# Four casts moved from VectorE to ScalarE, and three bias products moved ahead of a transpose, in the start-up of an attention-and-mixer kernel

## Chip, cores, metric

One core of a Trainium2 chip (trn2). The metric is the device time of one execution in microseconds (us), slowest core, here the only one. Lower is better.

## The reference

T5-style attention with a relative-position bias, then a mixer whose token mixing is low rank. Eight batches, eight heads, 576 tokens, head size 64; rank 32; hidden width 2048.

```python
def _attn_ref(q, k, v, bias_table):            # (8, 8, 576, 64)
    scores = scale * np.matmul(q, k.transpose(0, 1, 3, 2))
    ...                                        # bucket of |i - j|, 32 buckets
    scores = scores + bias.transpose(2, 0, 1)[None]
    attn = softmax(scores)                     # shortened
    return np.matmul(attn, v)

def _moe_ref(x, U, V, w_ch1, w_ch2):           # x: (8, 576, 512)
    h = x.transpose(0, 2, 1) @ U @ V           # U: 576 x 32, V: 32 x 576
    u = x + h.transpose(0, 2, 1)
    return u + np.maximum(u @ w_ch1, 0.0) @ w_ch2
```

## The kernel before

The kernel works through 32 "pairs" (batch, two heads). The bias is applied as a product after the exponential: `P = exp(scale * q k)` on ScalarE, then `P *= eb` on VectorE near the diagonal, where `eb` is a table of exponentiated biases that GpSimd (or VectorE) writes in reversed order. U and V are cast into zero-padded bf16 tiles `upad` and `vpad`. Batch 0 (pairs 0 to 3) is scheduled by hand, as the start-up is; from pair 4 on, score work is interleaved with the channel matmuls of earlier batches (the "dense" part). In all timelines shown here each engine's instructions stand in the order in which they are emitted.

```python
def cast_uv():                                   # the mixing weights
    nc.vector.tensor_copy(out=upad[:, 0:4, 0:R], in_=u_st[:, 0:4, :])
    for par in range(2):
        rows = slice(par * 64, par * 64 + 64)
        nc.vector.tensor_copy(out=upad[rows, 4 + par, 0:R], in_=u_st[rows, 4, :])
    nc.vector.tensor_copy(out=vpad[0:R, 0:S], in_=v_st)

# ... GpSimd's queue, in order
    load_w1(0)                                   # 1 MB with a cast on the way
    load_rem(1, 0)
    load_rem(1, 1)
    qk1 = [[load_pair(which, 0) for which in range(2)]]

    def more_loads():
        for pr in (2, 3):
            load_eb(pr)
        reverse_eb(2, nc.gpsimd.tensor_copy)     # table of pair 2
        load_w1(1)
        reverse_eb(3, nc.gpsimd.tensor_copy)     # table of pair 3
        # ... pair 1 of batch 1, v of batch 1, pairs 2 and 3, then load_w2 twice

# ... slot 1 and its neighbours
    kts(1, 2)                                    # a score tile of pair 1, with its exponential
    kts(1, 3)
    pvs(0, 4, 0, 1, 2, 3)                        # value products of pair 0 (PE)
    bands(1, 4, 0)                               # bias products of pair 1 (VectorE)
    cast_uv()
    normalise(0)
    rem_scores(2)
    kts(2, 0)
    first_transposes(3, qk0.pop(3), one)         # PE, then two copies on VectorE
    bands(1, 1, 2)
    first_rem_transposes(3)
    bands(1, 3)
    mix_t(0, nc.scalar.copy)                     # first reader of upad
    kts(2, 1)
    pvs(1, 4, 0, 1)
    kts(2, 2)
    pvs(1, 2, 3)
    ...
    bands(2, 4, 0, 1, 2, 3)

# batch 2's loads (GpSimd): remainders, then q and k in turn, then v
        for t in range(NKT):
            for which in range(2):
                seq.append(lambda which=which, t=t: main(which, t))
```

The softmax here doesn't subtract the row's maximum and nothing guards it: scores larger than these inputs give would overflow.

## Time and profile before

| | before |
|---|---|
| time, three runs | 409.25 us (408.82 to 409.63) |
| span of the profiled run | 407.1 us |
| PE idle in 24 to 30 us | 0.33 + 1.01 us |
| first dense slot (pair 4's first score matmul) | 38.47 us |
| PE waits for batch 2's q load | until 69.77 us, 0.52 us |

How to read it: PE is busy 95% of the time, so only PE's waits are worth anything. The views that carry this are in the prediction. Some lines that it names without showing them follow: GpSimd's timeline, VectorE's product of pair 2, the third exponential of pair 2 on ScalarE and PE's first dense slot (start, duration, engine, line, operation, output and inputs; in brackets the idle time before and its releaser).

```profile
27.72 0.74 POOL L265 DMA_DIRECT2D qb<-in_k_dram  x1 [4.37 <-DMA w1b<-in_moe_w_ch_dram]
28.46 0.84 POOL L213 COPY eb<-stage 128x768 bf16<-128x768 bf16 x1
...
28.06 1.57 DVE L587 TENSOR_TENSOR p_sb<-p_sb,eb 128x256 bf16<-128x256 bf16 x1
...
26.24 1.02 ACT L533 ACTIVATE p_sb<-sc 128x1024 bf16<-128x1024 f32 x1 [0.81 <-PE sc L524]
...
38.47 0.39 PE L537 MATMUL sc<-qkT 128*128 128x128 bf16 x4
```

GpSimd stands still for 4.37 us until the first half of `w1b` has landed, then issues one load, and only then makes the table for pair 2.

### The profile page before, as it was taken

How to read it: one execution, taken by the hardware profiler on the slowest of the kernel's cores; microseconds unless marked ns; L12 is line 12 of the kernel's file. 1: busy time of each engine (PE TensorE's matmuls, PEld its weight loads, DVE VectorE, ACT ScalarE, POOL GpSimd, SP SyncE). 2: the span in 40 equal slices, each digit the busy share in tenths (PEclk: the TensorE clock that was granted, in tenths of full speed). 3: DMA queues.
4: the chain of work that ended last, by engine and by line, in shares of the span. 5: the costliest groups of instructions: out<-in, count | busy, mean ns of one | idle time of the engine just before them, and what ended most of it. 6: DMA issues, size and time to landing. Idle time of an engine off the chain costs nothing.

```text
span 407.1 us, 9061 instructions
## 1 busy us (share of the span) xinstructions
PE 386.2 (95%) x3636; PEld 214.7 (53%) x3700; DVE 245.5 (60%) x558; ACT 205.7 (51%) x285; POOL 125.1 (31%) x179
## 2 busy tenths in 40 slices
PE   3889999999999999999999999999999999999995
PEld 1456555555555555555555555555555554444443
DVE  6987887758655675556755776558656832422321
ACT  4877644665654566556655665555554640220310
POOL 4958924454454045404540454040000000000000
PEclk9789999999999999999999999999999999999999
DMA  7999999999999699949996999499032003001012
GB/s 130 178 163 162 111 191 120 124 101 156 157 83 105 132 120 83 131 103 143 100 105 130 136 80 97 101 138 102 14 66 66 14 14 101 30 7 72 25 27 78
DMA packets 162754, 40.68 MB, mean 100 GB/s; under 512 B 151792, under 2 KB 157176, under 8 KB 162712
## 3 DMA queue, kind: packets, MB, share of 16 engines
q0 software_dynamic: 108416, 17.97, 61.1%
q1 hardware_dynamic: 53080, 21.22, 25.7%
q10 hardware_dynamic: 1216, 0.92, 0.8%
q8 instruction: 29, 0.48, 0.5%
q14 instruction: 13, 0.11, 0.1%
HBM read 37.84 MB, written 9.45 MB: 116 GB/s over the span
## 4 chain that ended last, share of the span: by engine, by line
PE 81%; DMA 11%; POOL 5%; issue 2%; DVE 1%; ACT 0%; DVEq 0%; POOLq 0%
PE acc L392 30%; PE acc L372 27%; PE o L611 10%; PE sc L524 7%; DMA w1b<-in_moe_w_ch_dram 4%; DMA w2b<-in_moe_w_ch_dram 3%; PE acc L647 2%; POOL v_bf L255 2%; PE acc L663 1%; POOL qb L265 1%; DMA qb<-in_q_dram 1%; PE sc L537 1%; PE sc L558 1%; DMA tblT<-in_bias_table_dram 1%; DMA gp_dram<-gp 1%
## 5 line engine op out<-in xcount | busy, mean ns | idle before, releaser
L533 ACT ACTIVATE p_sb<-sc 128x1024 bf16<-128x1024 f32 x128 | 124.5, 1021 | 100.9 <-PE sc L524 100.7
L392 PE MATMUL acc<-w2b,g 128*128 128x512 bf16 (+1 forms) x560 | 128.6, 373 | 2.3 <-DVE ob L401 0.5
L372 PE MATMUL acc<-uT,w1b 128*128 128x512 bf16 x484 | 116.3, 380 | 2.5 <-issue 0.6
L392 PEld LDWEIGHTS <-g 128*128 128x128 bf16 x592 | 55.1, 98 | 70.2 <-issue 11.7
L372 PEld LDWEIGHTS <-w1b 128*128 128x128 bf16 x576 | 53.2, 98 | 71.5 <-issue 13.1
L383 DVE TENSOR_SCALAR g<-acc 128x512 bf16<-128x512 f32 x94 | 64.7, 690 | 34.7 <-PE acc L372 31.7
L587 DVE TENSOR_TENSOR p_sb<-p_sb,eb 128x768 bf16<-128x768 bf16 (+3 forms) x160 | 71.1, 473 | 10.1 <-ACT p_sb L533 9.5
L381 ACT ACTIVATE g<-acc 128x512 bf16<-128x512 f32 x50 | 29.9, 598 | 59.9 <-PE acc L372 59.7
L611 PEld LDWEIGHTS <-p_sb 128*128 128x128 bf16 x1600 | 56.1, 98 | 7.0 <-issue 1.3
L611 PE MATMUL o<-v_bf,p_sb 128*128 128x65 bf16 x1500 | 58.0, 194 | 0.3 <-DVE p_sb L587 0.3
L401 DVE TENSOR_TENSOR ob<-acc,u_tok 128x512 f32<-128x512 f32 x32 | 22.1, 691 | 44.3 <-PE acc L392 41.7
L524 PE MATMUL sc<-qkT 64*128 64x512 bf16 x256 | 41.4, 392 | 1.2 <-ACT qkT L469 0.7
L915 POOL COPY gate<-xp 1x2 bf16<-1x2 bf16 x18 | 3.2, 176 | 121.5 <-DVE xp L636 121.5
L671 DVE TENSOR_TENSOR u_tok<-acc,xp 128x512 bf16<-128x512 f32 x32 | 22.1, 691 | 24.8 <-PE acc L663 24.7
L636 DVE TENSOR_TENSOR xp<-o,rcp 128x320 bf16<-128x320 f32 x60 | 29.5, 492 | 3.2
L255 POOL DMA_DIRECT2D v_bf<-in_v_dram x32 | 28.5, 914 | 1.9 <-DMA w1b<-in_moe_w_ch_dram 1.5
L255 POOL DMA_DIRECT2D qb<-in_k_dram x24 | 21.7, 906 | 5.5 <-DMA w2b<-in_moe_w_ch_dram 3.5
L255 POOL DMA_DIRECT2D qb<-in_q_dram x24 | 22.0, 915 | 4.7 <-DVE u_tok L671 4.7
L567 ACT ACTIVATE p_sb<-sc 128x640 bf16<-128x640 f32 x32 | 22.3, 698 | 0.2
L550 ACT ACTIVATE p_sb<-sc 128x512 bf16<-128x512 f32 x32 | 19.1, 597 | 4.7 <-PE sc L537 3.4
L634 DVE RECIPROCAL rcp<-o 128x5 f32<-128x5 f32 x60 | 11.4, 191 | 12.2 <-PE o L611 11.5
L647 PEld LDWEIGHTS <-upad 128*128 128x128 bf16 x160 | 11.4, 98 | 7.7 <-DVE xp L636 0.7
(90 smaller groups left out, 257.9 us busy)
## 6 DMA issues: line engine op xcount, KB each, us to landing
out_dram<-ob SPq DMA_DIRECT2D x32, 256.0 KB, 2.3
v_bf<-in_v_dram POOLq DMA_DIRECT2D x32, 128.0 KB, 5.8
qb<-in_q_dram POOLq DMA_DIRECT2D x27, 128.0 KB, 4.4
qb<-in_k_dram POOLq DMA_DIRECT2D x27, 128.0 KB, 4.4
w1b<-in_moe_w_ch_dram POOLq DMA_DIRECT2D x2, 1024.0 KB, 8.9
w2b<-in_moe_w_ch_dram POOLq DMA_DIRECT2D x2, 1024.0 KB, 12.1
stage<-gp_dram SPq DMA_DIRECT2D x4, 192.0 KB, 4.4
qkT<-qb SPq DMA_TRANSPOSE x40, 4.9
```

The lines of the kernel that those rows point to most:

```text
L255: nc.gpsimd.dma_start(out=dst, in_=src[b, :, t * 128 : (t + 1) * 128, :].rearrange("h p d -> p h d"),)
L372: nc.tensor.matmul(gp_, lhsT=w1b[:, ct, nt * 128 : (nt + 1) * 128], rhs=rhs[:, ct, :], start=(ct == 0), stop=(ct == 3),)
L381: nc.scalar.activation(g[:, nt, :], gp_, AF.Relu)
L383: nc.vector.tensor_relu(out=g[:, nt, :], in_=gp_)
L392: nc.tensor.matmul(op[:, c0:c1], lhsT=g[:, nt, tt * 128 : (tt + 1) * 128], rhs=w2b[:, nt, c0:c1], start=(nt == 0), stop=(nt == NHT - 1), s ...
L401: nc.vector.tensor_tensor(out=ob[:, c0:c1].rearrange("p (a c) -> p a c", c=128), in0=op[:, c0:c1].rearrange("p (a c) -> p a c", c=128), in ...
L524: nc.tensor.matmul(sp[:, hh, :], lhsT=kT[rows, i * 128 : (i + 1) * 128], rhs=qT[rows, 0:S0], start=True, stop=True,)
L533: nc.scalar.activation(P[:, i, :, 0:S0], sp, AF.Exp, scale=scale)
L567: nc.scalar.activation(P4[:, 0:SP], sp.rearrange("p a c -> p (a c)")[:, 0:SP], AF.Exp, scale=scale,)
L587: nc.vector.tensor_tensor(out=t, in0=t, in1=e, op=ALU.mult)
L611: nc.tensor.matmul(o[:, qt * 66 : qt * 66 + 65], lhsT=lhs[:, c0 : c0 + 128], rhs=rhs, start=(kt == NKT and qt == 0), stop=(kt == NKT - 1), ...
L636: nc.vector.tensor_tensor(out=xo[:, :, hh], in0=o[:, :, 0:64], in1=rbc, op=ALU.mult)
```

## The change

Intent: relieve VectorE in slot 1. The casts go to ScalarE, which has a hole there, and the rest of pair 1's bias products no longer wait behind the copies of pair 3's transposes.

```diff
     def cast_uv():
-        nc.vector.tensor_copy(out=upad[:, 0:4, 0:R], in_=u_st[:, 0:4, :])
+        nc.scalar.copy(out=upad[:, 0:4, 0:R], in_=u_st[:, 0:4, :])
         for par in range(2):
             rows = slice(par * 64, par * 64 + 64)
-            nc.vector.tensor_copy(out=upad[rows, 4 + par, 0:R], in_=u_st[rows, 4, :])
-        nc.vector.tensor_copy(out=vpad[0:R, 0:S], in_=v_st)
+            nc.scalar.copy(out=upad[rows, 4 + par, 0:R], in_=u_st[rows, 4, :])
+        nc.scalar.copy(out=vpad[0:R, 0:S], in_=v_st)
@@
     kts(1, 3)
+    cast_uv()
     pvs(0, 4, 0, 1, 2, 3)
     bands(1, 4, 0)
-    cast_uv()
     normalise(0)
     rem_scores(2)
     kts(2, 0)
+    bands(1, 1, 2, 3)
     first_transposes(3, qk0.pop(3), one)
-    bands(1, 1, 2)
     first_rem_transposes(3)
-    bands(1, 3)
```

## The prediction

> **What bounds the kernel now.** I read the page first: busy shares, the 40 slices, the chain that ended last.
>
> ```profile
> PE 386.2 (95%) x3636; PEld 214.7 (53%) x3700; DVE 245.5 (60%) x558; ACT 205.7 (51%) x285; POOL 125.1 (31%) x179
> PE   3889999999999999999999999999999999999995
> PE 81%; DMA 11%; POOL 5%; issue 2%; DVE 1%; ACT 0%; DVEq 0%; POOLq 0%
> ```
>
> TensorE (PE) is busy 95% of the 407.1 us span and carries 81% of the chain; VectorE (DVE), which the change relieves, carries 1%, ScalarE (ACT) 0%. So removing vector work is worth only what PE waits for it. Those waits can lie only where PE has gaps, so I read the busy table by windows next (columns: window, length, then busy us with instruction count of PE, PEld, DVE, ACT and POOL, then clock, DMA share, GB/s).
>
> ```profile
> 18.00:21.00 3.00, 3.00 (x48) 2.56 (x48) 2.93 (x11) 1.73 (x2) 3.00 (x6) 0.50 1.68 213
> 21.00:24.00 3.00, 2.80 (x41) 1.89 (x38) 1.92 (x6) 2.06 (x3) 2.29 (x4) 0.74 1.18 214
> 24.00:27.00 3.00, 2.67 (x57) 1.93 (x57) 2.61 (x7) 2.13 (x4) 0.00 (x0) 1.00 1.36 192
> 27.00:30.00 3.00, 1.99 (x20) 1.07 (x18) 2.94 (x6) 2.79 (x5) 2.28 (x4) 1.00 1.59 104
> 70.00:200.00 130.00, 128.47 (x1326) 72.97 (x1348) 84.54 (x192) 77.05 (x105) 54.24 (x78) 1.00 1.16 118
> ```
>
> From 70 us on PE is 99% busy (128.47 of 130). The changed code lies in slot 1, where pair 1 is weighted while pair 2's scores run: about 18 to 27 us. There PE is idle 0.2 us of 21 to 24 and 0.33 us of 24 to 27, with a further 1.0 us in 27 to 30. That is the whole local stake. From 18 to 21 the granted clock is 0.50, so PE is saturated on slow matmuls there.
>
> Third, the timelines of single engines around it. ScalarE, then VectorE, then TensorE (start, duration, what; in brackets the idle time before and its releaser):
>
> ```profile
> 17.80 1.94 ACT L533 ACTIVATE p_sb<-sc 128x1024 bf16<-128x1024 f32 x2
> 21.94 0.60 ACT L550 ACTIVATE p_sb<-sc 128x512 bf16<-128x512 f32 x1 [2.21 <-PE sc L537]
> ...
> 20.18 0.31 DVE L340 CAST upad<-u_st 128x128 bf16<-128x128 f32 x1
> 20.32 0.41 DVE L343 CAST upad<-u_st 64x32 bf16<-64x32 f32 x2
> 20.76 0.57 DVE L344 CAST vpad<-v_st 32x576 bf16<-32x576 f32 x1
> 21.26 0.17 DVE L634 RECIPROCAL rcp<-o 128x5 f32<-128x5 f32 x1
> ...
> 23.59 1.29 DVE L469 COPY qkT<-acc 128x512 bf16<-128x512 bf16 x2 [1.01 <-PE acc L465]
> 24.80 1.02 DVE L587 TENSOR_TENSOR p_sb<-p_sb,eb 128x768 bf16<-128x768 bf16 x2
> ...
> 25.40 0.32 PE L611 MATMUL o<-v_bf,p_sb 128*128 128x65 bf16 x5 [0.33 <-DVE p_sb L587]
> ```
>
> The reader sees three things: ScalarE has a hole of 2.21 us just where the four casts would go; VectorE sits idle 1.01 us ahead of the transposes' copies while three bias products wait behind them; and one PE wait of 0.33 us is for exactly such a product.
>
> Last, the chain of waits in order of time, 36 to 75 us, and the PE line where it returns to PE:
>
> ```profile
> 47.29 14.17 DMA w2b<-in_moe_w_ch_dram
> 61.46 0.30 issue
> 61.76 2.60 POOL qb L255 x3
> 64.36 5.37 DMA qb<-in_q_dram
> 69.72 0.05 issue
> ...
> 69.77 0.23 PE L498 MATMUL acc<-ident,qb 128*128 128x128 bf16 x1 [0.52 <-DMA qb<-in_q_dram]
> ```
>
> This is the decisive view. The chain ahead of 69.77 us is not PE at all: it runs through the GpSimd load queue (w1b, then v and qb loads, w2b, then batch 2's q), all the way back to the start. PE reaches batch 2's first transposes 0.52 us too early and waits for a load. Whatever PE gains before that point is waited away there, unless the load comes earlier too.
>
> **What the Trainium skill says.** (1) "ScalarE: Activation LUTs", section "What ACT_TABLE_LOAD costs": an activation with immediate scale and bias takes 186 ns plus 0.833 ns per element, consecutive ones overlap by about 93 ns. The trace agrees within 3%: 128x1024 from PSUM takes 1021 ns (formula 1039), 128x512 takes 597 (612). (2) Same page, "Table sets: the hidden batching unit": copy is in every set, so these casts should need no table switch between exponentials. The trace already mixes CAST and exp on ScalarE at 24 us (0.27 us, no gap). (3) "SBUF — State Buffer", "Who interferes with whom": a VectorE instruction with two SBUF inputs contends with a GpSimd instruction that reads SBUF, and the later one blocks. The trace is consistent: a 128x256 product that takes 0.28 us elsewhere lasts 1.57 us from 28.06, beside GpSimd's table copy from 28.46.
>
> **The change, part by part.**
> 1. *Casts off VectorE.* They occupy 20.18 to 21.33, 1.15 us. But the next VectorE instruction, the reciprocal of pair 0, needs head 0 of the value product, whose last matmuls end at 20.69 + 0.47 = 21.16 on PE. It started at 21.26. So about 0.1 us comes free, not 1.15.
> 2. *Casts onto ScalarE.* By the skill's formula (an estimate; no such cast from SBUF is in the trace): 128 elements 0.29, twice 32 elements 0.21, 576 elements 0.67, together 1.38, less three overlaps of 0.09 = 1.1 us. Queued after pair 1's exponentials they run from 19.74 to about 20.9 and end 1 us ahead of 21.94, when ScalarE's next work is released by PE. Cost on the path: 0. Their first reader, pair 0's mixing on PE, comes at 23.60.
> 3. *Three bias products ahead of pair 3's copies.* They start when pair 0's normalisation lets VectorE go, about 22.4, and last 1.02 + 0.48 less one overlap of 0.08 = 1.42 us, so end about 23.85. The copies wait for PE until 23.59 anyway; they move from 23.59 to 23.85, 0.26 us later, and end about 25.15; the small remainder copy ends about 25.35 instead of 26.0. Pair 3's scores need both only at 27.6.
> 4. *PE.* Its value products of pair 1 come at 24.30, 24.46, 24.61, 24.77, so the next without a wait is at 24.93, not 25.40: 0.47 us gained (idle plus restart). Pair 2's third score tile moves from 25.81 to 25.34, its exponential from 26.24 to 25.77 (the one before ends at 25.43). The 0.81 us hole before it on ScalarE shrinks to 0.35.
> 5. *What is left at the dense stage.* From 27.4 to 35 ScalarE is nearly solid, and would pass the 0.47 on. But pair 2's bias products need the table that GpSimd reverses at 28.46 to 29.30, released by the weight load that landed at 27.44; they run from 29.55 and cannot move ahead of about 29.35. They, pair 3's products and the two normalisations behind them keep about 0.2 us. The first dense slot, at 38.47 now, should start 0.2 to 0.4 us earlier; I take 0.25.
> 6. *At 69.77.* The load's landing doesn't depend on any of this, so PE arrives 0.25 us earlier and waits 0.77 instead of 0.52. Sum at the end: about 0. I put 0.15 us down for the chance that some of it survives: 409.25 - 0.15 = 409.1 us.
>
> **The rivals.** *The gain survives*: the load's chain shifts with PE, since one releaser in it (u_tok at 56.9, ahead of the load at 57.20) is VectorE work. For: it is on record as a wait of 4.7 us. Against: that releaser is no input of a q load, and w2b is what the next wait (3.5 us) names. Then 0.25 to 0.47 us stay: 408.8 to 409.0. *A new wait on ScalarE*: the landing of v_st isn't shown; if it came late, the casts would hold pair 2's exponentials. For: SyncE issued it only at 13.2 to 13.8. Against: VectorE read it at 20.76 without waiting, so ScalarE would end by 21.5 at worst. A delay of up to half a microsecond would be soaked up by the same wait at 69.77, so 409.2 to 409.5. *GpSimd is held*: the products move from 24.8, where GpSimd is idle, to 22.4, beside its DMA issues of 20.99 to 23.35. Against: it waits 4.37 us straight after, until 27.72, so a few tenths are lost in that. Also 409.2. *The delayed copies bind*: slack above 2 us, ruled out.
>
> **Range and chances.** All paths lie within half a microsecond, 0.12%; the three runs before spread over 0.8 us (408.82 to 409.63), and run-to-run variation of load landings and of PE's clock ramp is larger than the effect. Range 408.4 to 409.8. Over 2% either way (8 us) has no mechanism: 0.5% each.
>
> **What would show it.** Right: four short ScalarE casts between 19.7 and 21.1; the two-copy line at about 23.85 with no idle second before; no PE wait for p_sb at 25; third exponential near 25.8; first dense slot near 38.2; a PE wait for batch 2's qb load near 69.8 grown to about 0.8 us, PE in step with the kernel before afterwards. Wrong: that load lands earlier or the wait is gone and the span drops by 0.3 us or more (step 6 fails); casts past 21.94 (step 2); dense slot not earlier at all (step 5).

## The result, and the profile after

| | before | after |
|---|---|---|
| median (range) of 6 runs each | 409.5 us (408.82 to 410.27) | 409.25 us (408.49 to 409.94) |
| ratio after / before | | 0.9994, 95% interval 0.9978 to 1.0011 |
| span of the profiled run | 407.1 us | 408.0 us |
| first dense slot | 38.47 us | 38.59 us |
| PE waits for batch 2's q load | until 69.77, 0.52 us | until 70.68, 1.30 us |

A ratio is the mean time of one kernel's runs over that of the other's of the same rounds, so it is not quite the ratio of the medians. No change can be told from zero. Nor can a small one be ruled out: this interval, from 0.9 us faster to 0.5 us slower, would hide all of the 0.25 to 0.48 us that were at stake. What became of them must be read from the traces and the experiments.

The page's busy shares and chain after:

```profile
PE 386.7 (95%) x3636; PEld 214.8 (53%) x3700; DVE 243.2 (60%) x554; ACT 207.0 (51%) x289; POOL 124.7 (31%) x179
...
PE 81%; DMA 10%; POOL 5%; issue 2%; DVE 1%; ACT 0%; ACTq 0%; POOLq 0%
```

VectorE has four instructions fewer and ScalarE four more, the casts (1.3 us more of work there). The chain is what it was. ScalarE's timeline in slot 1, after, VectorE's below it, and PE's fifth group of value products of pair 1:

```profile
19.30 0.31 ACT L340 CAST upad<-u_st 128x128 bf16<-128x128 f32 x1
19.49 0.46 ACT L343 CAST upad<-u_st 64x32 bf16<-64x32 f32 x2
19.98 0.67 ACT L344 CAST vpad<-v_st 32x576 bf16<-32x576 f32 x1
21.64 0.60 ACT L550 ACTIVATE p_sb<-sc 128x512 bf16<-128x512 f32 x1 [0.99 <-ACT vpad L344]
...
25.63 1.02 ACT L533 ACTIVATE p_sb<-sc 128x1024 bf16<-128x1024 f32 x1 [0.32 <-PE sc L524]
...
22.16 1.42 DVE L587 TENSOR_TENSOR p_sb<-p_sb,eb 128x768 bf16<-128x768 bf16 x3
23.49 1.28 DVE L469 COPY qkT<-acc 128x512 bf16<-128x512 bf16 x2
27.45 0.28 DVE L587 TENSOR_TENSOR p_sb<-p_sb,eb 128x256 bf16<-128x256 bf16 x1
29.79 2.00 DVE L587 TENSOR_TENSOR p_sb<-p_sb,eb 128x512 bf16<-128x512 bf16 x3 [2.05 <-POOL eb L213]
...
24.80 0.32 PE L611 MATMUL o<-v_bf,p_sb 128*128 128x65 bf16 x5
```

Locally everything happened as intended. The casts sit in ScalarE's hole and end 0.99 us ahead of its next work. The third exponential of pair 2 moved from 26.24 to 25.63. (Not all of these 0.61 us are the change's: this trace runs ahead of the other already before the changed code has an effect on PE. PE's value products of pair 0 start at 18.20 against 18.50, those of pair 1 still at 24.18 against 24.30. Within the latter the fifth group starts 0.62 us behind the first, 24.80 - 24.18, where it was 1.10, 25.40 - 24.30. So 0.48 us are the change's.) In the busy table, the window of slot 1 is now solid on PE; the one after is as empty as it was:

```profile
24.00:27.00 3.00, 3.00 (x62) 2.09 (x60) 1.75 (x6) 2.50 (x4) 0.00 (x0) 1.00 1.43 187
27.00:30.00 3.00, 1.98 (x19) 1.07 (x18) 0.91 (x4) 2.91 (x5) 1.81 (x3) 1.00 1.30 88
```

Then it is lost. VectorE, ready at 27.73 for pair 2's remaining products, waits 2.05 us for GpSimd's table. GpSimd's timeline after, and the PE lines of the first dense slot and of the first wait for a load:

```profile
28.18 0.74 POOL L265 DMA_DIRECT2D qb<-in_k_dram  x1 [5.11 <-DMA w1b<-in_moe_w_ch_dram]
28.92 0.83 POOL L213 COPY eb<-stage 128x768 bf16<-128x768 bf16 x1
...
38.59 0.39 PE L537 MATMUL sc<-qkT 128*128 128x128 bf16 x4
70.68 0.23 PE L498 MATMUL acc<-ident,qb 128*128 128x128 bf16 x1 [1.30 <-DMA qb<-in_q_dram]
```

The gain meets two gates one after the other: the table of pair 2, made behind the load of `w1b`, and then batch 2's q load. Each is on GpSimd's queue; neither was touched.

### The profile page after: what moved, and what is told of

Read it like the earlier page. It is cut to its first block, busy times and chain, and to the rows that moved or that the text cites. A ratio compares the mean times of both kernels' runs of the same rounds, so it can differ in the third digit from the quotient of the medians.

```text
span 408.0 us, 9061 instructions
## 1 busy us (share of the span) xinstructions
PE 386.7 (95%) x3636; PEld 214.8 (53%) x3700; DVE 243.2 (60%) x554; ACT 207.0 (51%) x289; POOL 124.7 (31%) x179
## 4 chain that ended last, share of the span: by engine, by line
PE 81%; DMA 10%; POOL 5%; issue 2%; DVE 1%; ACT 0%; ACTq 0%; POOLq 0%
PE acc L392 30%; PE acc L372 27%; PE o L611 10%; PE sc L524 7%; DMA w1b<-in_moe_w_ch_dram 5%; DMA w2b<-in_moe_w_ch_dram 4%; PE acc L647 2%; POOL v_bf L255 2%; POOL qb L265 1%; PE acc L663 1%; DMA qb<-in_q_dram 1%; PE sc L537 1%; PE sc L558 1%; POOL qb L255 1%; DMA gp_dram<-gp 1%
## 5 line engine op out<-in xcount | busy, mean ns | idle before, releaser
L587 DVE TENSOR_TENSOR p_sb<-p_sb,eb 128x768 bf16<-128x768 bf16 (+3 forms) x160 | 69.8, 465 | 12.1 <-ACT p_sb L533 9.5
```

Source lines behind the costliest of these rows:

```text
L587: nc.vector.tensor_tensor(out=t, in0=t, in1=e, op=ALU.mult)
```

## The experiments

Twelve kernels, all giving the right result, each timed in five rounds against the kernel before on the same chip; the lines marked "L" shift by a few where a kernel has more lines. The three groups ran on three chips: compare within a group.

The theory: PE's work in the start-up doesn't set the time, because GpSimd's load chain does, at 70 us; and the change's local gain is already waited away at pair 2's table. Rivals: the gain is kept and noise hides it; one half of the change cancels the other; PE's work sets the end and nothing was gained at all.

### The kernel before, against itself

> The kernel before, unchanged, timed against itself: ratio 1.000, and the width of the interval is the noise that every other verdict is read against. It also gives a second trace: the theory (batch 2's q load, not PE, sets the time at 69.8 us) expects the same wait of PE for that load, with a landing that wanders by some tenths from run to run; the rival (that wait was an accident of one trace) expects it gone in some traces.

Measured: 409.75 us (before 409.8), ratio 1.0000 (0.9986 to 1.0013). So nothing below about 0.13% can be seen in these times, and where an interval is wider, nothing below its width. Its second trace (VectorE line, then PE line):

```profile
29.93 2.00 DVE L587 TENSOR_TENSOR p_sb<-p_sb,eb 128x512 bf16<-128x512 bf16 x3 [2.24 <-POOL eb L213]
70.63 0.23 PE L498 MATMUL acc<-ident,qb 128*128 128x128 bf16 x1 [1.13 <-DMA qb<-in_q_dram]
```

In this trace PE's clock was at full speed throughout slot 1, and the third exponential ran at 25.59, as early as in the trace after. The kernel before, too, then stands at the table and at the q load. The later landing in the trace after (70.68 against 69.77) needs no change to explain it: the kernel before shows it too (70.63).

### The change again

> The change, unchanged: ratio 0.9985 to 1.0005. The trace after showed the first dense slot at 38.59 us against 38.47 before although slot 1 had won 0.6 us on PE, because pair 2's bias products waited for GpSimd's table until 29.79. Theory: again a VectorE wait for that table of about 2 us near 27.5, and a PE wait for the q load near 70 us. Rival (the gain is kept and only that trace hid it): dense slot at 38.0 or earlier and the time 0.3 us or more below.

Measured: 410.34 us, ratio 1.0006 (0.9991 to 1.0022). The ratio lies a hair above the 0.9985 to 1.0005 that was expected, well within its interval; the trace isn't as expected. It fell in an execution whose first loads came late: PE waited for v until 20.81, its clock fell to 0.50 between 21 and 27 us, pair 1 was slow, and the first dense slot came at 40.61, later than the table would have allowed. In that trace no wait for the q load is left near 70 us. (The 0.6 us on PE that the expectation names are 0.48, as worked out above.) So the expectation of a 2 us wait for the table was a miss for this execution. It taught something else: a start-up later by 2 us cost the span (408.6 us) only 0.6 us against the other trace of the change.

### Only the casts

```diff
     kts(1, 3)
+    cast_uv()                                   # on ScalarE
     pvs(0, 4, 0, 1, 2, 3)
     bands(1, 4, 0)
-    cast_uv()                                   # on VectorE
```

> Only the four casts moved to ScalarE, the old order of products and transposes kept. Theory: they fill a hole on ScalarE and free about 0.1 us on VectorE ahead of a reciprocal that waits for PE; PE still waits 0.3 us for the product at 25.4; third score exponential still near 26.2; time within 0.1%. Rival (the casts were the costly part): exponential 0.5 us or more earlier.

Measured: 409.75 us, ratio 1.0003 (0.9987 to 1.0019). The PE line of the product in slot 1:

```profile
24.57 0.32 PE L611 MATMUL o<-v_bf,p_sb 128*128 128x65 bf16 x5 [0.32 <-DVE p_sb L587]
```

PE still waits 0.32 us there, as expected. The third exponential came at 25.41, and not near 26.2; taken alone that is what the rival forecast (0.5 us or more earlier). But this trace's clock was at 0.96 to full speed from 18 us on, where that of the kernel before had 0.50 and 0.74 until 24, and the kernel before, traced again at full speed, had it at 25.59 with no cast moved. So the spacing is compared, not the moment: the third exponential follows the first by 25.41 - 22.18 = 3.23 us, against 3.15 in the kernel before (26.24 - 23.09), 3.22 in its second trace (25.59 - 22.37) and 2.73 with the whole change (25.63 - 22.90). The casts alone don't help slot 1. The first dense slot was at 38.36, no later than with the whole change: slot 1's gain doesn't reach it.

### Only the order

```diff
     kts(2, 0)
+    bands(1, 1, 2, 3)
     first_transposes(3, qk0.pop(3), one)
-    bands(1, 1, 2)
     first_rem_transposes(3)
-    bands(1, 3)
```

> Only the bias products moved ahead of pair 3's transposes, casts left on VectorE. Theory: this half holds the whole local gain, PE's wait at 25 us gone, third exponential near 25.8 (0.45 us earlier); then VectorE waits for the table of pair 2, dense slot within 0.25 us of before, time within 0.1%. Rival (the delayed copies of pair 3 bind): scores of pair 3 later than 27.6 and the time longer.

Measured: 409.64 us, ratio 0.9998 (0.9981 to 1.0015). The time fits. The profiled execution was again one with late first loads (clock 0.50 in 24 to 27 us, first dense slot at 41.19), so the expected 25.8 of the exponential can't be checked. PE's wait for the product is gone in it (but at half the clock the products had more time). That this half holds the local gain rests on the difference between the whole change and the casts alone.

### Useless work on PE

Two, or fourteen, 512-column matmuls that nobody reads, just ahead of the first dense slot of the kernel before:

```diff
+    pad = acc()
+    for _ in range(2):                          # 14 in the second kernel
+        nc.tensor.matmul(pad, lhsT=ident, rhs=vpad[:, 0:S0], start=True, stop=True)
     put_off = [lambda g=g: mix_h(g) for g in range(NPAIR)]
```

> The kernel before with two useless 512-column matmuls (0.22 us each, about 0.43 us) on PE just ahead of the first dense slot. Theory (PE waits 0.5 to 1.3 us for batch 2's q load at 69.8): they come out of that wait, time within 0.1 us. Rival (PE work alone sets the end): 0.43 us longer.

> The same with fourteen such matmuls, 3.0 us. Theory: the wait at 69.8 us takes 0.5 to 1.3 us of it, the rest is seen: 1.7 to 2.5 us longer, and the wait for the q load is gone. Rival: 3.0 us longer.

Measured: two matmuls 409.4 us, ratio 0.9999 (0.9982 to 1.0016); fourteen 410.76 us, ratio 1.0039 (1.0025 to 1.0053), which is 0.0039 x 409.5 = 1.6 us for 3.0 us of work. PE lines: the wait that is left with two, then the padding with fourteen. Below them GpSimd's issue of batch 2's last q load with fourteen.

```profile
70.43 0.23 PE L498 MATMUL acc<-ident,qb 128*128 128x128 bf16 x1 [1.31 <-DMA qb<-in_q_dram]
...
38.49 3.19 PE L895 MATMUL acc<-vpad,ident 128*128 128x512 bf16 x14
...
64.54 0.90 POOL L255 DMA_DIRECT2D qb<-in_q_dram  x1
```

With two, the time can't decide: its interval, 0.7 us each way, is wider than the dose of 0.43. Fourteen settle the rival that PE's work alone sets the end: 3.0 us longer would be 1.0073, outside the interval. About 1.4 of the three microseconds vanish, and no wait for the q load near 70 us is left. They also answer the prediction's first rival, that the load's chain shifts with PE: with PE 3 us later from 38.49 on, the last q load was issued at 64.54, against 64.36 in the kernel before and 64.92 with two. (The VectorE instruction that is named as the releaser in that chain changes from trace to trace: u_tok, p_sb, g.) A PE time saved before 70 us is waited away there as long as that wait stands: the same wait, seen from the other side. (1.6 is a little under the 1.7 to 2.5 that was expected; the slack in these executions is at the upper end, and the interval is 0.6 us each way.)

### The q loads of batch 2 ahead of its k loads

```diff
-        for t in range(NKT):
-            for which in range(2):
-                seq.append(lambda which=which, t=t: main(which, t))
+        pairs = [(which, t) for t in range(NKT) for which in range(2)]
+        if b == 2:
+            pairs.sort()
+        for which, t in pairs:
+            seq.append(lambda which=which, t=t: main(which, t))
```

> The kernel before with batch 2's four q loads issued ahead of its four k loads (same loads, same bytes). The last q load is issued some 2.6 us earlier (three loads of 0.87 us). Theory: PE's wait for it, 0.5 to 1.3 us, goes, and the time drops by about that, 0.4 to 1.0 us; k lands about a microsecond later than it did, still ahead of its transposes 3 us on. Rival (another wait lies just behind): time within 0.2 us.

> The same reordering on top of the change. Theory: with the load out of the way the change is worth what the first dense slot gains: between 0 and 0.3 us below the reordered kernel before, since the table of pair 2 holds VectorE until about 29.5. Rival (the change's 0.5 us in slot 1 lasts once the load is gone): 0.5 us below it.

Measured: on the kernel before 408.61 us, ratio 0.9986 (0.9971 to 1.0001); on the change 408.57 us, ratio 0.9983 (0.9969 to 0.9997). PE in the second one, where it used to wait:

```profile
68.81 0.39 PE L500 MATMUL acc<-ident,qb 128*128 128x128 bf16 x4
69.03 0.22 PE L500 MATMUL acc<-ident,rem 128*128 128x128 bf16 x1
```

The wait is gone in this trace, and about 0.6 to 0.7 us of time with it; with the change on top the interval just excludes 1, without it it just includes it. (The trace without the change again had late first loads, first dense slot 40.20, so that it can't show the wait gone.) The two kernels can't be told apart, 0.04 us between the medians, which fits the theory that the first gate still stands; but with intervals of 0.6 us each way the times don't exclude the rival's 0.5 us. In the trace of the second one GpSimd's table started at 28.50 and the first dense slot came at 38.35, as in the kernels without this edit.

### The tables of pairs 2 and 3 made earlier

GpSimd makes both tables ahead of its loads for pair 0 of batch 1, when it would otherwise soon stand still, not after them.

```diff
-    qk1 = [[load_pair(which, 0) for which in range(2)]]
+    qk1 = []
     def more_loads():
         for pr in (2, 3):
             load_eb(pr)
         reverse_eb(2, nc.gpsimd.tensor_copy)
-        load_w1(1)
         reverse_eb(3, nc.gpsimd.tensor_copy)
+        qk1.append([load_pair(which, 0) for which in range(2)])
+        load_w1(1)
```

> The kernel before with GpSimd reversing the tables of pairs 2 and 3 ahead of the loads of pair 0 (at about 21 us), not behind the weight load that lands near 27.5. Theory: pair 2's products start when VectorE is free (about 28), not at 29.5 to 29.9, and GpSimd issues the second half of w1b about 0.8 us earlier, so the load chain behind it moves ahead too: PE's wait near 70 us shrinks by about that; time 0.3 to 1.0 us below. Rival (the load queue's room, not GpSimd's instructions, sets the landings): wait near 70 unchanged, time within 0.2 us.

> The same on top of the change. Theory: with the table there, slot 1's 0.5 us is no longer waited away near 27.5; dense slot at 37.5 to 38.1 in a trace whose clock comes up early; but the q load's wait near 70 us takes it, so the time is that of the early-table kernel before within 0.3 us. Rival (the table was the only thing that hid the gain): 0.5 us below it.

Measured: on the kernel before 410.6 us, ratio 1.0027 (1.0009 to 1.0046), that is 1.1 us slower; on the change 409.22 us, ratio 1.0002 (0.9986 to 1.0018). The first is a clear miss. Its VectorE line and its PE line in slot 1:

```profile
20.21 2.36 DVE L343 CAST upad<-u_st 64x32 bf16<-64x32 f32 x1
...
24.80 0.48 PE L647 MATMUL acc<-xp,upad 128*128 128x128 bf16 x5 [1.40 <-DVE xp L636]
```

A 64x32 cast that takes 0.18 to 0.19 us in the kernel before lasts 2.36 us here. It ends at 22.57, with GpSimd's two table copies, which run from 20.87 to 22.54. That the copies held it is read from these times. The casts end at 23.5, not 21.3; the normalisation of pair 0 behind them is late by the same 2 us; PE waits 1.40 us for it, and its clock falls (0.68 in 24 to 27 us). The first dense slot came at 40.57. With q loads first as well (below), the 128x128 cast took 0.92 us and a 64x32 one 1.53 us beside the same copies. The section that the prediction cites for two engines' contention for SBUF ("Who interferes with whom") names casts too among the instructions that can contend, in a mode that uses both of VectorE's ports. It was met where it wasn't looked for; whether these casts ran in that mode, no trace shows.

With the change there is no cast on VectorE to be held. PE and VectorE lines of that trace:

```profile
27.05 1.95 DVE L587 TENSOR_TENSOR p_sb<-p_sb,eb 128x256 bf16<-128x256 bf16 x5
...
37.46 0.39 PE L537 MATMUL sc<-qkT 128*128 128x128 bf16 x4
69.78 0.23 PE L498 MATMUL acc<-ident,qb 128*128 128x128 bf16 x1 [1.43 <-DMA qb<-in_q_dram]
```

All five products of pair 2 run from 27.05 without waiting, and the first dense slot comes at 37.46, 0.9 to 1.3 us earlier than in the other traces with a fast clock. The load chain moved ahead too (w1b's second half issued at 28.68, against 29.68), and the q load landed at 69.7. PE had stood waiting for 1.43 us by then. The time is unchanged (0.9 us less would be 0.9978, outside the interval): one gate opened, and the whole gain stands at the next. The expectation had put this kernel within 0.3 us of the one with early tables and without the change; it came 1.0 us below it in the mean of six runs each, which fits that only the other has casts on VectorE for the copies to hold.

### Both edits

> Early tables and q loads first, without the change. Theory: no wait for a q load near 70 us, PE solid from the dense slot on; 0.8 to 2.0 us below the kernel before (what q first gave, 0.6, plus what the tables give).

> Both on top of the change: both gates gone. Theory: here at last slot 1's gain reaches the end, 0.2 to 0.6 us below the same kernel without the change, 1 to 2.5 us below the kernel before; dense slot about 0.4 us earlier than without the change where both traces' clocks come up alike. Rival (something else in 27 to 38 us, ScalarE's solid stretch, hides it): the two within 0.1 us and the same dense slot.

Measured: without the change 409.5 us, ratio 1.0011 (0.9987 to 1.0035); with it 408.16 us, ratio 0.9986 (0.9956 to 1.0016). Neither differs clearly from the kernel before, and the runs scatter more than elsewhere (406.96 to 411.14 with the change). The first is a miss: it was expected 0.8 to 2.0 us faster, and the held casts are why it isn't; its trace shows PE's wait of 1.42 us for the normalisation again. The second has the fastest single run of all, 406.96 us, and a median 1.1 us below before, but it is no shown gain. A likely reason for the scatter, which no run took apart: once the load no longer holds PE, a late first load comes through to the end. Its profiled execution was a late one (PE waited for v until 20.70 and for k until 23.89, first dense slot 38.73), so the dense slot can't be compared as expected.

### The first dense slot follows the table

The start of GpSimd's copy for pair 2 and of the first dense slot in the traces whose clock was at full speed from 24 us on (the padding, 0.43 and 3.03 us, taken off its dense slot; the trace with both edits and the change is left out, since PE stood waiting for late loads in it):

| trace | table copy starts | first dense slot | difference |
|---|---|---|---|
| before | 28.46 | 38.47 | 10.01 |
| after | 28.92 | 38.59 | 9.67 |
| before, again | 29.06 | 38.72 | 9.66 |
| casts only | 28.69 | 38.36 | 9.67 |
| two useless matmuls | 28.68 | 38.34 | 9.66 |
| fourteen useless matmuls | 28.83 | 38.49 | 9.66 |
| q first, with the change | 28.50 | 38.35 | 9.85 |
| early tables, with the change | 20.71 | 37.46 | not bound |

In five traces, with and without the change, the dense slot stands 9.66 or 9.67 us behind the table. A sixth, q loads first without the change, whose clock was slow until 27 us, has 30.53 and 40.20: 9.67 again. There it is the table that sets it, and with the table made early the dense slot comes earlier. The two rows that stand out, the first trace and q first with the change, have the earliest tables of the old order, and VectorE's first product of pair 2 was still to come in them: it ran from 28.06 and 27.92, beside the copy, and lasted 1.57 and 1.75 us where the others have 0.28. It ended at 29.63 and 29.67, 0.33 us behind the copy. That was VectorE's to win in the first trace, and the change did win it: after, the same product ran at 27.45 in 0.28 us. But there the table came 0.46 us later.

## Why the prediction was right, point by point

- **Bound.** Right: PE's work before 70 us is not what ends last there. The fourteen useless matmuls show it in one direction, the reordered q loads, less clearly, in the other.
- **Step 1**, casts off VectorE are worth 0.1 us: right. In the trace after, VectorE stands idle 0.93 us before the reciprocal, which starts at 20.89, just as the value product's last matmuls end (20.86).
- **Step 2**, casts free on ScalarE: right. They took 1.35 us from 19.30, not 1.1, and still ended 0.99 us early. The landing of v_st did not hold them in any trace of the change.
- **Steps 3 and 4**, the products ahead of the copies win about 0.47 us on PE: right, in size too. On PE it was 0.48 us (1.10 - 0.62, above); by the spacing of exponentials 0.42 (3.15 - 2.73), or 0.49 against the second trace of the kernel before. The three products took the 1.42 us that were worked out.
- **Step 5**, "The first dense slot, at 38.47 now, should start 0.2 to 0.4 us earlier": wrong. It came at 38.59. The step knew the gate, but took the table to come at the same moment in every execution. It comes when the first half of w1b lands, and that wandered from 27.44 (before) to 27.90 (after) and 28.04 (before, again). The trace of before had the earliest of these, and so VectorE had something to win in it.
- **Step 6**, the q load takes what is left: right as to the gate, but in the trace after it had no gain to take. PE came to it 0.12 us later than before (69.04 against 68.92 for the matmuls ahead of the wait), not 0.25 earlier; the wait was 1.30 us, not 0.77, because the load landed 0.91 us later. That a gain does end there is shown by the early tables. In the five traces other than the first that show the wait, it was 1.13 to 1.43 us; the 0.52 us that the prediction started from was the smallest seen. In the executions with late first loads there was none.
- **A citation.** The prediction gives, from the skill, that the later of two contending instructions blocks, and calls the trace consistent. By the recorded starts it was the earlier one that was held: the product started at 28.06, the copy at 28.46, and likewise the cast at 20.21, the copies at 20.87. That the two engines hold each other up is what the trace shows, not in which order; spans on GpSimd are rough.
- **The sum**, 0.15 us of gain, can't be told from zero with intervals of 0.13%. The measured median is 409.25; within the range. That says little by itself: the range, 408.4 to 409.8, also holds no change at all and each rival's number. And it is luck that the sizes in steps 5 and 6, taken from a trace with an early table and a short wait, did no harm to the sum: the gain was lost one gate sooner than they had it.
- **The rivals.** "The gain survives" fell with the early tables, the first dense slot 0.9 us or more earlier and the time unchanged, and with the fourteen matmuls, which did not move the load. "GpSimd is held" didn't happen in the change, but its reverse did happen in an experiment: GpSimd held VectorE.

What stays open: whether the change is worth something once both gates are open. With early tables it is the difference between 410.6 and 409.22 us, which is shown, but that is because it takes the casts out of GpSimd's way. With both edits the scatter hides it. The only version whose interval lies below the kernel before is the change with the q loads first: 408.57 us, 0.17% below. It was not timed beside the change alone, and the q loads first without the change come to 408.61.

## What to carry to other kernels

Before a wait is removed, follow the path from it to the end and list every place where the engine will wait for something else anyway. At such a place a gain is lost whatever its size, a delay only up to the length of the wait; and one trace gives only one draw of that length. A dose of useless work, clearly larger than the noise, measures it directly. An engine move that gains nothing today can still be what makes another edit possible, as here, where the casts, left on VectorE, were caught by GpSimd's copies.

## What the Trainium skill lacked or had wrong

- "ScalarE: Activation LUTs", section "What ACT_TABLE_LOAD costs": the single durations fit these casts from SBUF well (0.31, 0.22 and 0.67 us; by the formula 0.29, 0.21 and 0.67). The overlap of 93 ns didn't hold for the short ones: two 64x32 casts together span 0.46 us, twice one of 0.22, and the four took 1.35 us, not the 1.1 that the formula and the overlap give.
- "SBUF — State Buffer", section "Who interferes with whom": it states the contention, and these runs agree (64x32 cast 0.19 us alone, 2.36 us beside two GpSimd copies of 0.9 us). What it doesn't say is that the delay can exceed the one GpSimd instruction in the way: here the cast outlasted both. It lets the one that issues first have the ports; by the recorded starts the held one was first (cast 20.21, copy 20.87; product 28.06, copy 28.46). Whether a recorded start is the moment of issue, no run shows.
- "DMA: Bandwidth & Descriptors", section "SWDGE vs HWDGE vs iDMA": it tells where the ring of GpSimd's loads lies, but not when a full one makes GpSimd stand still. In the traces with the old order of tables GpSimd waited 3.9 to 5.3 us before a 64 KB load, until an earlier load of a megabyte had landed, and everything else in its order, a table for VectorE included, waited with it. That the queue's room is the reason is an inference from the traces; no run took it apart.
